# Reordering the first two blocks of a fused chunk attention and MoE kernel: one load, some fillers, one product and one group moved

## The chip, the cores and the metric

One core of a Trainium2 chip (trn2) runs the whole program. The metric is the device time of one execution in microseconds; lower is better. The kernel before takes 287.46 us (median of the four runs that went with the changed kernel, 287.26 to 288.2). A difference counts as faster or slower from 2% on, which is 5.7 us here.

## The reference

```python
def _attn_ref(q, k, v):            # each (8, 8, 576, 64) float32
    # chunks of 64 rows: softmax(q k^T / 8) v inside each chunk
    ...
def _moe_ref(x, w_in, w_out, beta):  # x 4608 x 512, w_in 512 x 2048, w_out 2048 x 512
    h = x @ w_in
    g = h * (1.0 / (1.0 + np.exp(-beta * h)))
    return (g @ w_out).astype(np.float32)

x = attn_out.transpose(0, 2, 1, 3).reshape(B * S, H * D)   # 4608 tokens, 512 features
```

The two matrix products of the second part are nearly all of the work. Attention is worked on in units of 256 tokens (18 of them, two 128-token tiles each); the two products run in blocks of two units (512 tokens). The first product is called layer 1 here, and its 128-row slice m of a block is "m0", "m1" and so on. A bank is one of the buffers of PSUM, the memory that the matmuls write to; an eviction is the instruction of VectorE (DVE) that reads a layer-1 bank, writes the result to SBUF (the memory that the next matmul reads) and so frees the bank. Fillers are matmuls on zeros that only keep TensorE (PE) busy.

## The kernel before

The parts that the change and the argument touch (cuts are marked with `...`):

```python
ps_p = ctx.enter_context(tc.tile_pool(name="ps_p", bufs=4, space=bass.MemoryType.PSUM))  # layer-1 and output banks
ps_s = ctx.enter_context(tc.tile_pool(name="ps_s", bufs=1, space=bass.MemoryType.PSUM))  # one buffer: scores, products, transposes
ps_x = ctx.enter_context(tc.tile_pool(name="ps_x", bufs=1, space=bass.MemoryType.PSUM))  # one more such buffer
...
def emit_pv(u, where=("x", "s")):          # attention product of unit u, both tiles (PE)
    et = et_t.pop(u)
    for s in (1, 0) if u >= MU else (0, 1):
        ...
def emit_norm(u, s):                       # DVE: reciprocal, then multiply, out of PSUM
    ...
def emit_xt_pe(u, s, copy=nc.scalar.copy): # PE transposes of one tile, then one copy to SBUF
    xf = x16_t.pop((u, s)).rearrange("p r h d -> p (r h d)")
    tag = "s" if u < 2 and (u, s) != (1, 0) else "xp"[s]
    xp = {"x": ps_x, "s": ps_s, "p": ps_p}[tag].tile([128, 4, 128], FP16, tag=tag, name="xp")
    ...
def emit_m(j, m, c0=0, n=None, later=False):   # layer 1: 4 matmuls, tanh on ACT, eviction on DVE
    ...
    hps = ps_p.tile([128, 512], FP32, tag="p", name="hps")
    ...
def emit_t(j, t, k0=0, k1=None):               # layer 2; at the last k one copy on ACT and the store
    ...
with tc.manual_schedule():                     # order of emission is the order on each engine
    ...
    for i in range(4):
        load_v(i)
        ...
    make_identity(nc, ident)
    for g in range(8):
        load_w_in(g)
    ...
    emit_T_half(0); emit_sc_half(0, 0); emit_ex_half(0, 0)
    warm = idle_bank()
    emit_idle(6, 512, warm)                    # fillers: matmuls on zeros
    emit_T_half(1)
    nc.vector.transpose(out=bt, in_=braw)
    emit_sc_half(0, 1); emit_ex_half(0, 1); emit_sc_half(1, 0)
    ...
    emit_xt_pe(0, 0)
    emit_pv(1, ("x", "p"))
    emit_norm(1, 1)
    emit_norm(1, 0)
    nc.scalar.activation(out=beta2, in_=bt[:, 0:KFF], func=ACTF.Copy, scale=0.5)
    emit_xt_pe(0, 1)
    d = [emit_m(0, m, 0, 256, True) for m in (0, 1)]
    d[0][0]()                                  # tanh of m0
    emit_xt_pe(1, 1)
    d[1][0]()
    d.append(emit_m(0, 2, 0, 256, True))
    d[0][1]()                                  # eviction of m0 (DVE) ahead of the copy below
    emit_xt_pe(1, 0, nc.vector.tensor_copy)
    d.append(emit_m(0, 3, 0, 256, True))
    ...
    for m in range(4):
        emit_m(0, m, 256, 256)                 # the second half-block: moment S
    ...
    # block 0's layer 2 in 16 groups; unit 2, unit 3 and block 1's first pieces in between
    for i in range(16):
        ...                                    # scores of 2 at 8, product of 2 at 10, scores of 3 at 14
        if i == 15:
            a0, v0 = emit_m(1, 0, 0, 256, True); a0()
            emit_pv(3); emit_norm(3, 0); emit_norm(3, 1)
            v0()
            emit_m(1, 1, 0, 256)
        emit_t(0, i % 4, 4 * (i // 4), 4 * (i // 4) + 4)
    emit_xt_pe(3, 0)
    emit_m(1, 2, 0, 256)
    emit_xt_pe(3, 1)
    emit_m(1, 3, 0, 256)
    emit_m(1, 4, 0, 256)
    for m in range(5, KFF):
        emit_m(1, m)                           # the first full group: moment F
```

The softmax here doesn't subtract the row's maximum and nothing guards it: scores larger than these inputs give would overflow.

## Time and profile before

| | before |
|---|---|
| time, median | 287.46 us |
| span of the profiled execution | 285.8 us |
| TensorE (PE) busy | 279.2 us, 98% |
| VectorE (DVE), ScalarE (ACT) busy | 143.6 and 146.2 us |
| M, first layer-1 matmul | 15.16 us |
| S, second half-block of layer 1 starts | 17.59 us |
| F, first full group of block 1 starts | 49.48 us |

M, S and F are three moments on PE's timeline. PE is full after F (218.95 of 218.95 us in this execution), so what is lost or won ahead of F is lost or won for good. Of the waits of PE (the view lists who waited for whom, us in total, times, longest), these are the ones after the first fillers, and they are short (about 0.25 us more ahead of S and as much ahead of F do not reach this view, because the ends of matmuls are modelled):

```profile
PE hps L329 <- ACT xt L304: 0.7, 1, 0.7
PE x L266 <- ACT et L208: 0.2, 1, 0.2
```

A timeline line reads: start, length, engine, line of the kernel, operation, output<-input, sizes, count, and in brackets the idle time of that engine before it with what ended it. The stretches and timelines on which the argument rests are in the prediction.

### The profile page before, as it was taken

Reading aid. Unit: us, or ns where it says so; the run is one execution under the profiler, and the core shown is the slowest. Engines: PE = TensorE matmul, PEld = TensorE weight load, DVE = VectorE, ACT = ScalarE, POOL = GpSimd, SP = SyncE. Lnnn points to the kernel's source line nnn. Section 1 sums busy time; section 2 is a strip of 40 time slices with the busy share of each in tenths; the row PEclk is TensorE's granted clock in tenths of the full one; section 3 lists DMA queues with packets and bytes.
Section 4 is the critical chain, followed back from the end, with each engine's and each line's share of the span. In section 5 each row is a group of like instructions: output and inputs, shape, how many; then the busy total and the mean of one; then the engine's idle time right before and its main releaser. Section 6 shows DMA issues by size and latency. Waiting matters only on the chain.

```text
span 285.8 us, 6671 instructions
## 1 busy us (share of the span) xinstructions
PE 279.2 (98%) x2779; PEld 136.5 (48%) x2779; DVE 143.6 (50%) x268; ACT 146.2 (51%) x223; POOL 95.6 (33%) x125
## 2 busy tenths in 40 slices
PE   6989999999999999999999999999999999999995
PEld 3564456544544444444444444444444444444444
DVE  2678444776558553535454536363635463333301
ACT  4478228773557545455554555554546444444411
POOL 8853678488073991168607000000000000000000
PEclk9999999999999999999999999999999999999999
DMA  8999999999999999999999983425311221010012
GB/s 198 177 197 206 182 179 213 209 164 150 207 104 173 178 176 162 170 190 187 168 170 164 174 130 78 100 57 119 79 54 39 73 57 55 37 39 37 37 73 76
DMA packets 141085, 37.40 MB, mean 131 GB/s; under 512 B 128000, under 2 KB 136576, under 8 KB 141056
## 3 DMA queue, kind: packets, MB, share of 16 engines
q0 software_dynamic: 99136, 17.83, 82.3%
q1 hardware_dynamic: 41776, 19.09, 32.5%
q8 instruction: 22, 0.36, 0.5%
q10 hardware_dynamic: 144, 0.07, 0.1%
q14 instruction: 7, 0.06, 0.0%
HBM read 36.71 MB, written 9.44 MB: 161 GB/s over the span
## 4 chain that ended last, share of the span: by engine, by line
PE 96%; POOL 1%; ACT 1%; issue 1%; DVE 0%; DVEq 0%; POOLq 0%
PE hps L329 44%; PE ops L361 43%; PE warm L381 2%; PE x L266 2%; PE sc L238 1%; PE ops L602 1%; PE sc L225 1%; PE y L266 1%; ACT xt L304 1%; POOL h L401 1%; PE sc L198 1%; POOL vbig L113 1%; PE xp L303 0%; ACT et L208 0%; PE xp L311 0%
## 5 line engine op out<-in xcount | busy, mean ns | idle before, releaser
L343 DVE SCALAR_TENSOR_TENSOR gt<-sg,hps 128x512 f16<-128x512 f32 (+1 forms) x153 | 99.2, 655 | 101.9 <-ACT sg L339 101.3
L329 PE MATMUL hps<-xt,win 128*128 128x512 f16 (+1 forms) x612 | 136.2, 367 | 0.8 <-ACT xt L304 0.7
L339 ACT ACTIVATE sg<-hps,beta 128x512 f32<-128x512 f32 (+1 forms) x153 | 100.4, 662 | 71.3 <-PE hps L329 69.7
L361 PE MATMUL ops<-wout,gt 128*128 128x512 f16 x560 | 131.1, 379 | 0.0
L329 PEld LDWEIGHTS <-win 128*128 128x128 f16 x612 | 58.3, 98 | 62.4 <-issue 1.0
L361 PEld LDWEIGHTS <-gt 128*128 128x128 f16 x560 | 54.1, 98 | 64.0
L371 ACT ACTIVATE osb<-ops 128x512 f32<-128x512 f32 x35 | 20.9, 598 | 42.8 <-PE ops L361 42.8
L113 POOL DMA_DIRECT2D vbig<-in_v_dram x40 | 34.0, 867 | 11.9 <-DMA wout<-in_moe_w_out_dram 3.6
L99 POOL DMA_DIRECT2D qu<-in_q_dram x22 | 18.7, 859 | 24.9 <-DMA qT<-qu 22.5
L287 DVE TENSOR_TENSOR x<-x,rd 128x512 f16<-128x512 f32 x27 | 18.7, 691 | 1.0
L99 POOL DMA_DIRECT2D ku<-in_k_dram x22 | 18.7, 874 | 0.9 <-DMA ku<-in_k_dram 0.9
L285 DVE RECIPROCAL rd<-x 128x8 f32<-128x8 f32 x27 | 5.4, 199 | 13.1 <-PE x L266 13.1
L247 ACT ACTIVATE et<-sc 128x1024 f16<-128x1024 f32 (+1 forms) x8 | 6.4, 811 | 8.7 <-PE sc L238 8.7
L231 ACT ACTIVATE et<-sc 128x1024 f16<-128x1024 f32 x10 | 10.2, 1021 | 0.7
L266 PEld LDWEIGHTS <-et 64*64 64x64 f16 x576 | 6.0, 107 | 7.4 <-issue 4.7
L381 PE MATMUL warm<-idle 128*128 128x512 f16 (+1 forms) x32 | 8.0, 401 | 0.0
L287 DVE TENSOR_TENSOR x<-y,rd 128x256 f16<-128x256 f32 x18 | 7.6, 424 | 0.6
L105 POOL DMA_DIRECT2D ku<-in_k_dram x9 | 6.8, 755 | 2.6 <-DMA win<-in_moe_w_in_dram 1.3
L105 POOL DMA_DIRECT2D qu<-in_q_dram x9 | 6.8, 766 | 1.5 <-DMA win<-in_moe_w_in_dram 0.7
L266 PE MATMUL x<-vbig,et 64*64 64x65 f16 x432 | 6.7, 194 | 0.2 <-ACT et L208 0.2
L614 DVE TENSOR_SCALAR osb<-ops 128x256 f32<-128x256 f32 (+1 forms) x2 | 0.7, 358 | 12.1 <-PE ops L602 12.1
L131 POOL DMA_DIRECT2D win<-in_moe_w_in_dram x8 | 6.0, 767 | 1.4 <-DMA vbig<-in_v_dram 1.4
(46 smaller groups left out, 75.3 us busy)
## 6 DMA issues: line engine op xcount, KB each, us to landing
out_dram<-osb SPq DMA_DIRECT2D x35, 256.0 KB, 3.6
vbig<-in_v_dram POOLq DMA_DIRECT2D x32, 128.0 KB, 7.8
qu<-in_q_dram POOLq DMA_DIRECT2D x20, 128.0 KB, 5.7
ku<-in_k_dram POOLq DMA_DIRECT2D x20, 128.0 KB, 7.4
win<-in_moe_w_in_dram POOLq DMA_DIRECT2D x8, 256.0 KB, 8.9
wout<-in_moe_w_out_dram POOLq DMA_DIRECT2D x4, 512.0 KB, 12.2
qu<-in_q_dram POOLq DMA_DIRECT2D x3, 256.0 KB, 7.4
ku<-in_k_dram POOLq DMA_DIRECT2D x3, 256.0 KB, 7.9
```

The costliest lines, as they stand in the source:

```text
L99: nc.gpsimd.dma_start(out=tv[off:off + n, sp], in_=src[b, :, s:s + n, :].rearrange("h p d -> p h d"),)
L105: nc.gpsimd.dma_start(out=t[off // 2:(off + n) // 2], in_=src[b, :, s:s + n, :].rearrange("h (p r) d -> p h r d", r=2),)
L113: nc.gpsimd.dma_start(out=vbig[off:off + n, i, :, 0:D], in_=v[b, :, s:s + n, :].rearrange("h p d -> p h d"),)
L231: nc.scalar.activation(out=et, in_=sc, func=ACTF.Exp, scale=scale)
L266: nc.tensor.matmul(out=(x[0][64 * c:64 * c + 64, r, g, 0:D + 1] if len(x) == 1 else x[r][64 * c:64 * c + 64, g, 0:D + 1]), lhsT=(et[64 * r ...
L287: nc.vector.tensor_tensor(out=o, in0=z[..., 0:D], in1=rd[:, r].to_broadcast(list(o.shape)), op=ALU.mult)
L329: nc.tensor.matmul(out=hps[:, 0:n], lhsT=w_in16[m // 2][:, kk, (m % 2) * 128:(m % 2) * 128 + 128], rhs=xr[:, c0 // CH:(c0 + n) // CH, 2 * ...
L339: nc.scalar.activation(out=sg[:, 0:n], in_=hps[:, 0:n], func=ACTF.Tanh, scale=beta2[:, m:m + 1])
L343: nc.vector.scalar_tensor_tensor(out=gt_t[j][:, m, c0:c0 + n], in0=sg[:, 0:n], scalar=1.0, in1=hps[:, 0:n], op0=ALU.add, op1=ALU.mult,)
L361: nc.tensor.matmul(out=ops, lhsT=gt_t[j][:, kk, t * 128:(t + 1) * 128], rhs=w_out16[kk // 4][:, kk % 4, :], start=(kk == 0), stop=(kk == K ...
L371: nc.scalar.activation(out=osb, in_=ops, func=ACTF.Copy, scale=0.5)
L381: nc.tensor.matmul(out=d[:, 0:w], lhsT=idle[:, 0:128], rhs=idle[:, 0:w])
```

## The change

Its intent, as far as the edit tells it: get the first w_in piece into SBUF earlier, let PE reach layer 1 earlier (fewer fillers, half of unit 1's product put behind m0), and in block 1 finish layer 2's last group ahead of unit 3's product so that its bank and its output copy are out of the way. The diff:

```diff
-    def emit_pv(u, where=("x", "s")):
-        et = et_t.pop(u)
-        for s in (1, 0) if u >= MU else (0, 1):
+    def emit_pv(u, where=("x", "s"), which=None):
+        et = et_t[u]
+        for s in which or ((1, 0) if u >= MU else (0, 1)):
 ...
-        tag = "s" if u < 2 and (u, s) != (1, 0) else "xp"[s]
+        tag = ("ss", "sx")[u][s] if u < 2 else "xp"[s]
 ...
+            if i == 2:
+                load_w_in(0)
 ...
-        for g in range(8):
+        for g in range(1, 8):
             load_w_in(g)
 ...
-        emit_idle(6, 512, warm)
+        emit_idle(3, 512, warm)
 ...
-        emit_idle(12, 64, warm)
+        emit_idle(15, 64, warm)
         emit_xt_pe(0, 0)
-        emit_pv(1, ("x", "p"))
-        emit_norm(1, 1)
+        emit_pv(1, ("p", "x"), (0,))
         emit_norm(1, 0)
 ...
-        d = [emit_m(0, m, 0, 256, True) for m in (0, 1)]
+        d = [emit_m(0, 0, 0, 256, True)]
+        emit_pv(1, ("p", "x"), (1,))
+        emit_norm(1, 1)
         d[0][0]()
-        emit_xt_pe(1, 1)
-        d[1][0]()
+        d.append(emit_m(0, 1, 0, 256, True))
+        emit_xt_pe(1, 0)
         d.append(emit_m(0, 2, 0, 256, True))
-        d[0][1]()
-        emit_xt_pe(1, 0, nc.vector.tensor_copy)
+        emit_xt_pe(1, 1, nc.vector.tensor_copy)
         d.append(emit_m(0, 3, 0, 256, True))
-        for act, _ in d[2:]:
+        for act, _ in d[1:]:
             act()
-        for _, vec in d[1:]:
+        for _, vec in d:
             vec()
 ...
-            if i == 8:
+            if i == 9:
                 emit_sc(2)
-            if i == 10:
+            if i == 11:
                 emit_pv(2)
 ...
-            if i == 14:
+            if i == 15:
                 emit_sc(3, True)
-            if i == 15:
                 a0, v0 = emit_m(1, 0, 0, 256, True)
                 a0()
-                emit_pv(3)
-                emit_norm(3, 0)
-                emit_norm(3, 1)
                 v0()
-                emit_m(1, 1, 0, 256)
             emit_t(0, i % 4, 4 * (i // 4), 4 * (i // 4) + 4)
+        a1, v1 = emit_m(1, 1, 0, 256, True)
+        a1()
+        emit_pv(3)
+        emit_norm(3, 0)
+        v1()
+        emit_norm(3, 1)
+        emit_m(1, 2, 0, 256)
         emit_xt_pe(3, 0)
-        emit_m(1, 2, 0, 256)
+        emit_m(1, 3, 0, 256)
         emit_xt_pe(3, 1)
-        emit_m(1, 3, 0, 256)
         emit_m(1, 4, 0, 256)
```

## The prediction

> **What bounds the kernel now.** I read the page first (which engine is full), then the chain of work that ended last in order of time (where that engine is not full), then the busy time by stretch, then each engine's timeline around the two places that the diff touches. The stretches (start, end, length, then busy time of PE, PEld, DVE, ACT, POOL; granted clock, DMA share, GB/s):
>
> ```profile
> 0.00:17.59 17.59, 14.41 (x335) 8.38 (x335) 9.55 (x25) 8.47 (x14) 13.31 (x23) 1.00 1.40 189
> 17.59:49.48 31.89, 31.79 (x357) 16.94 (x357) 18.04 (x34) 17.96 (x32) 20.66 (x27) 1.00 1.64 195
> 49.48:268.43 218.95, 218.95 (x1992) 103.15 (x1992) 113.92 (x206) 117.02 (x174) 61.64 (x75) 1.00 1.14 121
> ```
>
> From 49.48 us on PE is never free until the tail, and the diff leaves that part alone. So whatever the change does is the shift of two moments: **S**, when the second half-block of layer 1 starts (17.59 now; before it PE runs fillers and short pieces), and **F**, when the first full 512-column group of block 1 starts (49.48). Later matmuls only move along with F. The start, from the timelines of PE, ACT and DVE:
>
> ```profile
> 11.66 0.32 PE L266 MATMUL x<-vbig,et 64*64 64x65 f16 x16
> 13.47 0.58 ACT L304 COPY xt<-xp 128x512 f16<-128x512 f16 x1
> 14.10 0.38 PE L303 MATMUL xp<-ident,x 128*128 128x128 f16 x4
> 15.16 1.03 PE L329 MATMUL hps<-xt,win 128*128 128x256 f16 x8 [0.67 <-ACT xt L304]
> 16.36 0.42 DVE L343 SCALAR_TENSOR_TENSOR gt<-sg,hps 128x256 f16<-128x256 f32 x1 [0.22 <-ACT sg L339]
> 17.11 0.42 DVE L304 COPY xt<-xp 128x512 f16<-128x512 f16 x1 [0.33 <-PE xp L303]
> ```
>
> See that the transposes of tile 1 (14.10) start as the copy of tile 0 leaves their buffer (13.47 + 0.58 = 14.05), that layer 1 starts 0.06 us after the next copy (14.52 + 0.58), and that DVE frees the first layer-1 bank (16.36) before it makes the copy that S waits for (17.11 + 0.42 = 17.53). The second place:
>
> ```profile
> 45.61 0.45 PE L266 MATMUL x<-vbig,et 64*64 64x65 f16 x32
> 45.99 0.21 DVE L285 RECIPROCAL rd<-x 128x8 f32<-128x8 f32 x1 [3.27 <-PE x L266]
> 46.23 0.69 DVE L287 TENSOR_TENSOR x<-x,rd 128x512 f16<-128x512 f32 x1
> 46.84 0.20 DVE L285 RECIPROCAL rd<-x 128x8 f32<-128x8 f32 x1
> 47.07 0.69 DVE L287 TENSOR_TENSOR x<-x,rd 128x512 f16<-128x512 f32 x1
> 47.51 0.60 ACT L371 ACTIVATE osb<-ops 128x512 f32<-128x512 f32 x1 [0.39 <-PE ops L361]
> 48.14 0.39 PE L303 MATMUL xp<-ident,x 128*128 128x128 f16 x4
> 48.83 0.60 ACT L304 COPY xt<-xp 128x512 f16<-128x512 f16 x1
> ```
>
> Unit 3's product starts at 45.61; its second tile is normalised at 47.76; the transposes wait a further 0.38 us, until the last output copy (47.51 + 0.60 = 48.11) frees their bank; the copy ends at 49.43 and F follows. Adding the PE work from group 14 (44.21) to F (in us: two groups at 0.86, four first-half pieces m1 to m4 and m0 at 0.43 each, a product 0.38, two transposes at 0.22, without the scores ahead of it) gives 4.69 of 5.27: about half a microsecond of PE is lost here, and about 0.25 just before S. That is nearly all there is to win; 2% of 287.4 would be 5.7 us.
>
> [...] eight 256-column matmuls take 15.16 to 16.03, 109 ns each. [...] The trace's fillers go from 0.43 us each (eight in 3.43, up to 8.41) to 0.22 by 9.31[...]. [...] Landings in this trace, issue start plus time to landing, keep the issue order: v tiles 0 to 3 at 11.05, 11.5, 12.15, 13.06; first and second w_in piece at 14.26 and 15.6. The first of these rows:
>
> ```profile
> vbig<-in_v_dram POOLq DMA_DIRECT2D x1, 128.0 KB, 8.2
> ```
>
> It was issued at 2.85. Landing reaches an engine in under 0.1 us: PE loads its first w_in weight at 14.34.
>
> **The change, part by part.**
>
> *Loads.* v tile 3 and w_in piece 0 swap. Spacings are about 0.9 us for a v tile and 1.2 to 1.35 for a w_in piece, so w_in 0 should land near 13.4 and v tile 3 near 14.3. Piece 1 stays at 15.6, with v tiles 0 and 1 unmoved. w_in 0 was not yet late (14.34 against 15.16), so alone this wins nothing; it is what allows an earlier start.
>
> *Fewer idles.* Three of six fillers go: 3 x 0.22 = 0.65 us. The second half scores need the last DVE transpose (8.74 + 1.07 = 9.81), so they start at 9.85 instead of 10.48. Their exponential ends at 10.96 instead of 11.59, but then unit 0's product waits for v tile 0 (about 11.13 instead of 11.66) and its second half for v tile 1 (about 11.58 instead of 11.81). So of 0.63 us only 0.3 passes: the scores behind it start 11.73 instead of 12.04, the exponential ends 13.26 instead of 13.57, the copy of tile 0 ends 13.74 and the next transposes start 13.79, the copy of tile 1 ends 14.79, and layer 1 starts at 14.84 instead of 15.16. The three added 64-column fillers (0.09 us) lie ahead of that wait.
>
> *Layer 1 ahead of the product.* From 14.84: m0 0.43, the product's other half from 15.29, m1, transposes of unit 1 tile 0 and m2 (from 16.1, after w_in 1). DVE starts on the product's result 0.38 us after its start, as in every row of L266/L285: 15.67, reciprocal to multiply 0.24, multiply 0.69, ends 16.60. Transposes 16.64, DVE copy 0.42 later (17.06 to 17.48). Now the evictions of m0 to m3 all come behind this copy in DVE's order; the first ends at 17.06 + 0.34 + 0.42 = 17.82. There are four layer-1 banks and m0 to m3 hold them, so the second half-block waits for it: S = 17.87 instead of 17.59. **Part sum: +0.3 us.**
>
> *Block 1 a group later.* Scores and product of unit 2 and the scores of unit 3 each move one group; the same work in another order, and no wait appears (normalised unit 2 at 42.20, its transposes at 42.16 to 42.61). Then, counted without part 1: group 14 ends 44.43, scores to 45.07, m0 to 45.50, group 15 to 46.37, m1 to 46.80, unit 3's product at 46.85 instead of 45.61: 1.24 us later. Reciprocal 47.23, multiply 47.47 to 48.16. Then DVE first evicts m1 (about 48.1 to 48.5), then reciprocal 48.43, multiply 48.70 to 49.40. Transposes 49.44, copy 49.86 to 50.45, F about 50.49. PE has only m2, m3, m4 and two transposes behind the product (1.73 us) against a chain of 3.6. The earlier output copy (about 47.25 instead of 48.11) does remove the bank wait of 0.38 and ACT's queue of 0.27. Sum: +1.24 + 0.4 (m1's eviction between the two normalisations) - 0.65 = **+1.0 us**.
>
> Total 287.4 + 0.3 + 1.0 = 288.7.
>
> **Rivals.** (1) The intent works: w_in 0 early starts layer 1 at 14.5 and S is at 17.3, and moving group 15 ahead clears the bank and ACT waits so that F falls at 49.0. For it: both waits exist in the trace. Against: the chain behind the product still needs 3.6 us. Time 286.6 to 287.0. (2) The shifts cancel: the early gain of 0.6 passes whole if v tile 0 lands sooner, but S then stays at 17.55, because the copy and the eviction follow each other on DVE; block 1 costs less as m1's eviction fits beside a wait. Time 287.4 to 288. (3) DMA becomes the bound: v tile 3 or w_in 1 lands late and PE stands for a microsecond; the DMA row is at 9 throughout, but no matmul now waits for a load and the bytes ahead of w_in 1 are the same. Time 289.5.
>
> **Range and chances.** My sums hold best for block 1, since the same constants reproduce the 49.48 of now; the start is less certain by 0.4 us. Weighting rival 2 a little, I put 288.5 us, 287.3 to 289.4. The runs of the kernel before spread 0.9 us. Nothing above reaches 5.7 us: faster by over 2% 0.01, within 2% 0.98, slower 0.01.
>
> **What would show it.** In the changed trace: first layer-1 matmul near 14.8; a PE gap of about half a microsecond before the second half-block, ended by DVE (eviction of m0); unit 3's product about 1.2 us later than before against group 14, then PE gaps before both its transposes, ended by DVE multiplies, and before F, ended by an ACT copy; 1.2 us or so more idle PE up to F, and equal time from F to the end. Wrong if F comes no later than 49.5 (the chain is shorter than I count, for instance the eviction of m1 ran earlier), or if the start gains over 0.3 us (the banks are not what S waits for).

## The result

The changed kernel takes 289.07 us (median of four runs, 288.81 to 289.34) against 287.46 us before. The ratio is 1.0051 with a 95% interval of 1.003 to 1.0072. Ratios here are the mean time of one kernel's runs over the mean of the other's runs of the same rounds, so they are not quite the ratio of the medians. The output is correct. By the 2% rule this is "same", and clear of the noise it is about half a per cent slower. The spans of the two profiled executions are 285.8 and 287.1 us.

The stretches of the changed kernel, cut at its own S and F:

```profile
0.00:17.89 17.89, 14.08 (x335) 8.08 (x336) 9.56 (x25) 8.70 (x14) 13.54 (x24) 1.00 1.39 189
17.89:50.82 32.93, 31.98 (x357) 16.75 (x358) 18.31 (x35) 18.54 (x32) 20.43 (x27) 1.00 1.63 196
50.82:269.74 218.92, 218.92 (x1993) 103.00 (x1992) 113.58 (x205) 116.61 (x173) 61.64 (x75) 1.00 1.11 120
```

The third stretch is as long as before (218.92 against 218.95), so the loss is all ahead of F. The first is 0.30 us longer with less PE work in it, and the second 1.04 us longer (32.93 against 31.89). Among the waits of PE that the kernel before does not have, these two are the longest:

```profile
PE xp L303 <- DVE x L287: 0.7, 2, 0.4
PE hps L329 <- DVE gt L343: 0.4, 1, 0.4
```

The timelines at the start (PE, ACT and DVE):

```profile
13.06 0.59 ACT L304 COPY xt<-xp 128x512 f16<-128x512 f16 x1
...
13.70 0.38 PE L303 MATMUL xp<-ident,x 128*128 128x128 f16 x4 [0.20 <-ACT xt L304]
...
14.75 0.60 PE L329 MATMUL hps<-xt,win 128*128 128x256 f16 x4 [0.67 <-ACT xt L304]
...
17.08 0.42 DVE L304 COPY xt<-xp 128x512 f16<-128x512 f16 x1 [0.49 <-PE xp L303]
17.43 1.43 DVE L343 SCALAR_TENSOR_TENSOR gt<-sg,hps 128x256 f16<-128x256 f32 x4
...
17.89 1.37 PE L329 MATMUL hps<-xt,win 128*128 128x256 f16 x11 [0.41 <-DVE gt L343]
```

In this pair of executions layer 1 starts 0.41 us earlier (14.75 against 15.16), yet S is later. The four evictions of m0 to m3 come in one run of DVE after its copy: m0's tanh had ended at 15.92 (15.45 + 0.47 on ACT), DVE stood 0.49 us ahead of the copy, and the eviction of m0 still ran only behind it, at 17.43. PE stands 0.41 us until the first of them frees a bank. In block 1, first PE's timeline, then DVE's:

```profile
47.21 0.45 PE L266 MATMUL x<-vbig,et 64*64 64x65 f16 x32
...
48.58 0.40 PE L303 MATMUL xp<-ident,x 128*128 128x128 f16 x4 [0.38 <-DVE x L287]
...
49.75 0.40 PE L303 MATMUL xp<-ident,x 128*128 128x128 f16 x4 [0.34 <-DVE x L287]
...
50.82 4.49 PE L329 MATMUL hps<-xt,win 128*128 128x512 f16 x26 [0.24 <-ACT xt L304]
```

```profile
47.83 0.69 DVE L287 TENSOR_TENSOR x<-x,rd 128x512 f16<-128x512 f32 x1
48.44 0.41 DVE L343 SCALAR_TENSOR_TENSOR gt<-sg,hps 128x256 f16<-128x256 f32 x1
48.76 0.20 DVE L285 RECIPROCAL rd<-x 128x8 f32<-128x8 f32 x1
49.00 0.69 DVE L287 TENSOR_TENSOR x<-x,rd 128x512 f16<-128x512 f32 x1
```

Unit 3's product starts 29.32 us after S (47.21 - 17.89), where it started 28.02 us after S before (45.61 - 17.59). PE then waits three times: for each normalised tile and for the last copy. Between the two multiplies DVE evicts m1.

### The profile page after: what moved, and what is told of

Read it like the earlier page. It is cut to its first block, busy times and chain, and to the rows that moved or that the text cites. A ratio compares the mean times of both kernels' runs of the same rounds, so it can differ in the third digit from the quotient of the medians.

```text
span 287.1 us, 6670 instructions
## 1 busy us (share of the span) xinstructions
PE 279.0 (97%) x2779; PEld 135.9 (47%) x2779; DVE 143.5 (50%) x268; ACT 146.6 (51%) x223; POOL 95.6 (33%) x125
## 4 chain that ended last, share of the span: by engine, by line
PE 93%; DVE 2%; DMA 1%; ACT 1%; issue 0%; DVEq 0%
PE hps L329 44%; PE ops L361 42%; PE x L266 2%; DMA raw<-in_q_dram 1%; PE sc L238 1%; PE ops L605 1%; PE sc L225 1%; DVE t L179 1%; PE y L266 1%; PE xp L303 1%; ACT xt L304 1%; DVE x L287 0%; PE sc L198 0%; ACT h L178 0%; ACT et L208 0%
## 5 line engine op out<-in xcount | busy, mean ns | idle before, releaser
L381 PE MATMUL warm<-idle 128*128 128x512 f16 (+1 forms) x32 | 7.3, 378 | 0.0
```

What stands on the lines that cost most here:

```text
L381: nc.tensor.matmul(out=d[:, 0:w], lhsT=idle[:, 0:128], rhs=idle[:, 0:w])
```

## The experiments

Twelve runs were made: ten edits, the unedited changed kernel again, and one edit twice. All gave the right output. The early loads and the pace of PE's fillers move M by up to half a microsecond from one execution to the next (14.75 and 15.21 in the two profiles of the changed kernel, 15.16 and 15.67 in two with the old start), so the table gives the differences between marks, which hardly scatter: M itself, S - M, F - S, then the median time and the ratio to the kernel before.

| run | what it is | M | S - M | F - S | time | ratio (95%) |
|---|---|---|---|---|---|---|
| before | | 15.16 | 2.43 | 31.89 | 287.46 | 1 |
| changed | | 14.75 | 3.14 | 32.93 | 289.07 | 1.0051 (1.003 to 1.0072) |
| after_again | changed, unedited | 15.21 | 3.13 | 32.93 | 289.25 | 1.0059 (1.0041 to 1.0077) |
| e1_start_only | only the start changed | 14.70 | 3.14 | 31.89 | 288.22 | 1.0016 (1.0002 to 1.0029) |
| e2_block_only | only block 1 changed | 15.67 | 2.43 | 32.92 | 289.11 | 1.0045 (1.003 to 1.0059) |
| e3_evict_first | changed, eviction of m0 ahead | 14.67 | 2.81 | 32.92 | 289.01 | 1.0045 (1.0031 to 1.006) |
| e4_norm_first | changed, m1's eviction behind | 15.19 | 3.13 | 33.10 | 288.92 | 1.004 (1.0025 to 1.0055) |
| e9_dve_orders | both of these | 15.17 | 2.81 | 32.61 | 288.55 | 1.0031 (1.0018 to 1.0045) |
| e5_loads_back | changed, loads as before | 16.78 | 3.13 | 32.93 | 289.38 | 1.0058 (1.0044 to 1.0071) |
| e5_again | the same again | 14.94 | 3.13 | 32.93 | 289.15 | 1.0053 (1.0039 to 1.0068) |
| e10_no_fillers | changed, no fillers there | 15.08 | 3.14 | 32.92 | 289.78 | 1.0101 (1.0063 to 1.0139) |
| e6_idles_only | before, three fillers fewer | 14.95 | 2.44 | 31.88 | 287.49 | 0.9993 (0.9981 to 1.0006) |
| e7_bank_free | before, other bank and copy engine | 15.41 | 2.44 | see below | 287.05 | 0.9982 (0.9967 to 0.9996) |
| e8_both | both, and both transposes ahead of m2 | 14.96 | no wait at S | see below | 287.09 | 0.9974 (0.9959 to 0.9989) |

The theory under test: the start and block 1 each lose on their own; at the start because the eviction of m0 stands behind a copy in DVE's order while PE needs its bank, in block 1 because a fixed chain (product, normalise, transpose, copy) begins 1.3 us later with too little matmul work beside it, and m1's eviction lengthens it.

### e1_start_only and e2_block_only: the two halves of the change

```diff
 e1: the changed kernel, but
-            the tests of i (9, 11, 15) and the lines from a1, v1 = ... to emit_m(1, 3, 0, 256)
+            the same lines of the kernel before
 e2: the kernel before, with those lines of the changed kernel
```

> Only the changes up to block 0's second half (loads swapped, fewer idles, product split, DVE order); block 1 as in the kernel before. Theory A (DVE's first-in-first-out order makes the second half-block wait for the eviction of m0, which now stands behind the copy): S at 17.89, F at 49.48 + 0.30 = 49.78, time 0.3 us above the kernel before (287.8), so ratio about 1.001. Rival B (the start is where the whole loss arises, block 1's different timing is only its echo): F above 50.5 and time near 289. Rival C (the start gains and the trace's 0.3 is a fluke of that run): S at or below 17.6, time at or below 287.4.

> Only block 1's scores, product and group moved; the start as in the kernel before. Theory A (the product of unit 3 comes 1.3 us later and its chain of normalise, transpose, copy has too little matmul work beside it): S 17.59, F 49.48 + 1.04 = 50.5, time 1.0 us above the kernel before (288.5), ratio about 1.0036; gaps of PE before both transposes of unit 3, ended by DVE multiplies. Rival B: F near 49.5 and no loss, since it came from the start.

Measured: the two halves separate cleanly. The start alone has the changed kernel's S - M (3.14) and the old F - S (31.89); block 1 alone has the old S - M (2.43) and the new F - S (32.92). e1's S was 17.84 and its F 49.73. e2's S was 18.10 rather than the 17.59 expected, though its start is the old code: its six fillers took 2.13 us instead of 1.64, which is the pace of PE's fillers, taken up below. In time, e1 is slower by 0.16% and e2 by 0.45%; these add to 0.61%, against the 0.51% and 0.59% of the two series of the changed kernel. Rival B (block 1 only echoes the start) is out, and so is rival C (S at or below 17.6).

### e3_evict_first, e4_norm_first and e9_dve_orders: two instructions of DVE

```diff
 e3 (and e9)
         d.append(emit_m(0, 2, 0, 256, True))
+        d[0][1]()
         emit_xt_pe(1, 1, nc.vector.tensor_copy)
 ...
-        for _, vec in d:
+        for _, vec in d[1:]:
 e4 (and e9)
         emit_norm(3, 0)
-        v1()
         emit_norm(3, 1)
+        v1()
```

> The changed kernel with one DVE instruction moved: the eviction of m0 ahead of the copy of unit 1's second tile. Theory A: the eviction runs at about 16.5 to 16.9, in DVE's gap before the copy (17.08 to 17.50), so S falls from 17.89 to about 17.56 and the time by 0.33 us (288.7 against 289.07). Rival D (S waits for the tanh or for a weight load, not for the bank that DVE frees): S stays at 17.9.

> The changed kernel with one DVE instruction moved: the eviction of m1 of block 1 behind the normalisation of unit 3's second tile. Theory A: that normalisation ends 0.3 us earlier (about 49.35 instead of 49.70), the transposes and the copy follow, F falls from 50.82 to about 50.45, unless m4, whose bank that eviction frees, then holds it (m4 could start at 49.75 at the earliest, F at 50.2: no). Time 0.35 us below the changed kernel (288.7). Rival E (the gap before the second transposes is set by something else): F stays at 50.8.

> The changed kernel with both DVE instructions moved (eviction of m0 ahead of the copy, eviction of block 1's m1 behind the second normalisation). Theory A: S - M 2.8 instead of 3.14, F - S 32.6 instead of 32.93, together 0.65 us off the changed kernel of the same submission, ratio to the kernel before about 1.0022. If the remaining loss is the later product itself, 0.7 us of F - S stays, whatever DVE's order.

Measured: e3's S - M falls by 0.33 us to 2.81, as expected; so the bank that DVE frees is what S waits for in the changed kernel. Its time (289.01) does not resolve a third of a microsecond. e4 missed its expectation on the face of it: F - S rose to 33.10. The trace shows why. In that execution PE paused within unit 3's 64 score matmuls (45.70 to 46.00 in the chain, with no wait that the profile shows), and the scores took 1.13 us instead of 0.64. From the product to F, e4 took 3.29 us (51.42 - 48.13) against the changed kernel's 3.61 (50.82 - 47.21), so the 0.32 us is there, but hidden. e9 settles it, with both edits and no pause. DVE's timeline of e9:

```profile
16.92 0.41 DVE L343 SCALAR_TENSOR_TENSOR gt<-sg,hps 128x256 f16<-128x256 f32 x1
17.50 0.42 DVE L304 COPY xt<-xp 128x512 f16<-128x512 f16 x1 [0.16 <-PE xp L303]
...
48.52 0.20 DVE L285 RECIPROCAL rd<-x 128x8 f32<-128x8 f32 x1
48.75 0.69 DVE L287 TENSOR_TENSOR x<-x,rd 128x512 f16<-128x512 f32 x1
```

The eviction now fits into the gap that DVE had ahead of its copy, and the second reciprocal follows the first multiply (which starts at 47.91) at once. S - M is 2.81 and F - S 32.61, together 0.65 us less than the changed kernel. In time e9 has 288.55 us against 289.25 for the unedited changed kernel, 0.70 us less. What is left of F - S, 32.61 - 31.89 = 0.72 us, goes by this account to the later product, whatever DVE's order; no run moves the product alone. What is left of S - M, 2.81 - 2.43 = 0.38 us, comes with the split of unit 1's product: half of it (0.25 us, 15.28 to 15.53 in the changed kernel) now runs between M and S, and in e9 S (17.98) waits for DVE's copy (17.50 + 0.42 = 17.92), which depends on that half. Nor did the split bring M nearer: from unit 0's second scores to M it is 4.68 us before (15.16 - 10.48), 4.69 in e6 below, where the product is whole, and 4.72 to 4.87 in the two profiles of the changed kernel.

### e5_loads_back and e5_again: does the load swap matter?

```diff
-            if i == 2:
-                load_w_in(0)
 ...
-        for g in range(1, 8):
+        for g in range(8):
             load_w_in(g)
```

> The changed kernel with the load order of the kernel before (v of tile 3 ahead of the first w_in piece). Theory A (the swap moves a transfer that nobody waits for): w_in 0 lands near 14.3 instead of 13.5, before layer 1 can start (14.75, set by the copy of tile 1), S stays at 17.9 and F at 50.8, time equal to the changed kernel within 0.2 us (289.0). Rival F (the swap is what lets layer 1 start early, as the change's wording suggests): layer 1 starts later than 14.9 and waits for a DMA, time 289.2 or more.

> The load order put back in the changed kernel, once more: its first profile fell on a run in which the second half of q and k landed 0.7 us late and TensorE then ran at the slow pace, so that look could not tell. Theory A (nobody waits for the swapped transfer): in a look without that, M 14.75, first w_in weight loaded by 14.4, S 17.9, time as the changed kernel's of the same submission within 0.3 us. Rival F (the swap is needed): the first layer-1 weight load is ended by a DMA, M above 15.0 though the copy of tile 1 ended earlier.

Measured: the first look could not tell (M at 16.78, for another reason, in the next part). In e5_again the first layer-1 weight load did wait for the transfer, but only until 14.43, and M was then set by the copy of tile 1 at 14.94, as in every other run. PE's weight loads in e5_again:

```profile
14.43 0.10 PEld L329 LDWEIGHTS <-win 128*128 128x128 f16 x1 [0.34 <-DMA win<-in_moe_w_in_dram]
```

The changed kernel loads that weight at 13.86. So the swap brings the piece half a microsecond earlier to a place where the next matmul waits for something else; e5_again's time (289.15) and after_again's (289.25) do not differ. By these figures it would matter only if M could get below about 14.5 (an estimate from the 14.43).

### e6_idles_only and e10_no_fillers: what the fillers do

```diff
 e6: the kernel before          e10: the changed kernel
-        emit_idle(6, 512, warm)    -        emit_idle(3, 512, warm)
+        emit_idle(3, 512, warm)
```

> The kernel before with three fillers fewer and nothing else. Theory A: layer 1 starts at about 14.75 as in the changed kernel, but DVE still evicts m0 before its copy, so S follows at about 17.2 (14.75 + 2.43), 0.4 us ahead of the kernel before; F about 49.07; time 287.1 to 287.3, ratio 0.9985. Rival G ([...] the early start runs into w_in 0): S at 17.6 or later, ratio 1 or above.

> The changed kernel with none of the three fillers left, so that TensorE stands from about 8.9 to 9.85. Theory H [...]: the 64-column fillers and transposes after it take the long durations (fillers over 0.05 us each, transposes 0.59 instead of 0.39), layer 1 starts at 15.5 or later, time 1 us or more above the changed kernel. Rival I (fillers at that place only waste time): M 14.7, time equal to the changed kernel within 0.2 us.

Measured: e6's S - M is the old 2.44, with m0 evicted ahead of the copy, so its S (17.39) is earlier than before (17.59), by 0.2 us instead of the expected 0.4. The step that was off is the fillers' pace. PE's timeline of e6, then of the changed kernel:

```profile
8.92 1.41 PE L381 MATMUL warm<-idle 128*128 128x512 f16 x3
```

```profile
8.88 0.82 PE L381 MATMUL warm<-idle 128*128 128x512 f16 x3
```

Three identical fillers took 1.41 us in one execution and 0.82 in the other: PE reached its fast pace (0.22 us for such a filler, against 0.43 at the slow one) at different moments. The granted clock of the profile does not show this: it reads 1.00 from 4.84 to 8.35 us in the kernel before, where the fillers took 0.43 us each, and 1.00 from 9.30 to 10.40, where they took 0.22. What sets the moment is not shown; fast and slow pace mean here only what the matmuls took. The time of e6 (ratio 0.9993) is not to be told from the kernel before; its profiled execution, the slowest of its six, also lost half a microsecond after F, in two pauses of PE near 95.6 and 155.2 us.

The question behind e10 was whether the slow pace, which followed a gap of 1.20 us in e5_loads_back, also follows another gap of about a microsecond at that place. Its expectation missed: with no fillers, its profile shows a gap of 1.13 us and the fast pace after it. M was 15.08 because its scores waited for DVE's last transposes, and these for the second half of k, which landed at 2.12 + 6.8 = 8.92 us. That load landed at 8.6 in the profile of the changed kernel and at 9.32 in after_again. But e5_loads_back had the other outcome after a gap of 1.20 us (its load landed at 2.12 + 7.35 = 9.47). PE's timelines, e5_loads_back first, then e10_no_fillers:

```profile
8.24 0.45 PE L198 MATMUL sc<-t,t 32*64 32x64 f16 x32
...
10.63 0.71 PE L198 MATMUL sc<-t,t 32*64 32x64 f16 x64 [1.20 <-DVE bt L433]
...
13.24 1.41 PE L381 MATMUL warm<-idle 128*128 128x512 f16 x16
14.45 0.59 PE L303 MATMUL xp<-ident,x 128*128 128x128 f16 x4
```

```profile
8.35 0.64 PE L198 MATMUL sc<-t,t 32*64 32x64 f16 x32
10.12 0.71 PE L198 MATMUL sc<-t,t 32*64 32x64 f16 x64 [1.13 <-DVE bt L434]
...
12.30 0.83 PE L381 MATMUL warm<-idle 128*128 128x512 f16 x16
12.96 0.39 PE L303 MATMUL xp<-ident,x 128*128 128x128 f16 x4
```

The same sixteen fillers took 1.41 us at the slow pace and 0.83 at the fast one, the same four transposes 0.59 and 0.39. That execution of e5_loads_back had a mean granted clock of 0.992 and took 291.05 us, 1.7 us above its fellows. Two of the four runs of e10 took 290.28 us (clock 0.992) and 292.16 (0.998), and one of after_again 290.31 (1.0). The kernel before never took more than 288.34 us in the twelve runs listed with the first eight experiments and the ten with the last four. So fewer fillers leave the start open to a late load (with six of them, in e7 below, the load landed as late, at 2.13 + 7.2 = 9.33, and PE did not wait for it), and in one profile the slow pace followed. Why one gap brings it and another of nearly the same length does not stays open, as do the runs that were not profiled. One difference: ahead of its gap, e5_loads_back was already at the fast pace (the 32 scores at 8.24 took 0.45 us) and turned slow near 11.5 us, about 3.3 us after it had turned fast, until about 14.9 (estimates from its timeline: two fillers at 11.28 took 0.87 us against 0.60 in e10, 32 scores at 12.66 took 0.64, and 16 product matmuls at 14.98 again 0.32); in e10 the scores ahead of the gap were still slow (0.64 us). No run varies this alone.

### e7_bank_free and e8_both: what the kernel before could still win

```diff
 e7 and e8, on the kernel before
-        tag = "s" if u < 2 and (u, s) != (1, 0) else "xp"[s]
+        tag = "s" if u < 2 and (u, s) != (1, 0) or (u, s) == (3, 1) else "xp"[s]
 ...
         emit_xt_pe(3, 0)
-        emit_m(1, 2, 0, 256)
-        emit_xt_pe(3, 1)
+        a2, v2 = emit_m(1, 2, 0, 256, True)
+        a2()
+        emit_xt_pe(3, 1, nc.vector.tensor_copy)
+        v2()
 e8 besides
-        emit_idle(6, 512, warm)
+        emit_idle(3, 512, warm)
 ...
-        d.append(emit_m(0, 2, 0, 256, True))
         d[0][1]()
         emit_xt_pe(1, 0, nc.vector.tensor_copy)
+        d.append(emit_m(0, 2, 0, 256, True))
```

> The kernel before with the last transposes of unit 3 put into the buffer that its own product has just left (no wait for the last output copy) and their copy given to DVE ahead of the eviction of m2. Theory A (the half microsecond that block 1 lost before came from that bank and from ACT's queue): transposes at about 48.0, copy about 48.4 to 48.8, F at 49.05 to 49.1 instead of 49.48, PE without a gap from the product to F; time 0.4 us below the kernel before, ratio 0.9986. Rival: F stays at 49.4 since the copy of unit 3's first tile or the evictions hold it.

> The kernel before with three fillers fewer, both transposes of unit 1 ahead of m2, and the block 1 edit of the bank-free run. Theory A: S at about 16.95 to 17.0 (PE-bound from the first layer-1 matmul at 14.75: four pieces 0.43 and two transposes 0.22 are 2.16), F 31.5 us later at about 48.5, so 1.0 us ahead of the kernel before; time 286.4 to 286.7, ratio 0.9966. Rival: the gains do not add, as the later matmuls then meet loads that land no earlier, F above 49.

Measured: in e7 no wait is left in block 1. PE's timeline of e7, where the transposes and the layer-1 pieces follow each other without a gap:

```profile
47.58 0.39 PE L303 MATMUL xp<-ident,x 128*128 128x128 f16 x4
47.80 0.60 PE L329 MATMUL hps<-xt,win 128*128 128x256 f16 x4
48.24 0.39 PE L303 MATMUL xp<-ident,x 128*128 128x128 f16 x4
48.46 1.25 PE L329 MATMUL hps<-xt,win 128*128 128x256 f16 x9
```

As F is no wait there, take the distance from S to the start of the last 48 matmuls: 278.65 - 17.85 = 260.80 us in e7, 278.79 - 17.59 = 261.20 before. That is the 0.40 us that was expected, and the time agrees (ratio 0.9982, 287.05 us). So what the kernel before lost here was the bank and ACT's queue (e7 lifts both at once and does not tell them apart), and both can be avoided without moving the product.

e8 has the best ratio, 0.9974, and beats both kernels, but not by the microsecond that was expected. PE has no gap from M to S. In the profiled execution, however, M was 14.96 (the fillers ran slow again, 1.38 us), and from M to the last 48 matmuls it took 263.62 us, against 263.24 in e7 and 263.63 before. Set against e7's timeline group by group, e8 is 0.58 us ahead when layer 2 of block 0 starts and loses that lead in steps: 0.24 us in unit 3's scores (0.90 us in the chain against 0.66), 0.06 near 68 us and 0.25 near 154 us. None of these shows a wait. They are not e8's alone: e4 paused within the same 64 scores, and e3 and e6 at the same step from layer 2 to layer 1 as e8 near 154 us (155.8 and 155.2 there, about 105.5 us after F in e8 and e3). What PE stands for at these places, in some executions and not in others, is open; e8 and e7 cannot be told apart by their times.

### after_again: the yardstick

> The changed kernel again, unedited, as the yardstick for the other runs of this submission and for how far its marks scatter. All theories: S - M (second half-block minus first layer-1 matmul) 3.14, F - S 32.93, time 1.3 us above the kernel before, ratio 1.0045; M between 14.6 and 15.3 [...].

Measured: as expected, except that the ratio is a little higher (1.0059), with the one run of 290.31 us in it. S - M and F - S repeat to 0.01 us while M moves from 14.75 to 15.21.

## Why the prediction was right

The prediction said 288.5 us with 287.3 to 289.4, and "within 2%"; the kernel took 289.07. It holds by its own steps, though not every close figure is skill: the moments M, S and F themselves move by half a microsecond between executions of the same kernel (after_again has 15.21, 18.34 and 51.27), so that they were met to 0.1 us in the one profile is partly luck. The distances S - M and F - S, the causes, and the times are what count.

- **M.** Predicted 14.84, seen at 14.75, and at 15.21 in after_again, where the second half of k landed late. Of the 0.60 us by which the scores start earlier (9.88 against 10.48), 0.41 arrive at M. That the loads of v eat part of it is right, but in this profile less than predicted: the product's first half starts at 11.06 instead of the predicted 11.13, as its exponential ends (10.39 + 0.60), since v tile 0 had landed at 2.86 + 8.0 = 10.86; the second half starts at 11.34 instead of 11.58, some 0.13 us later than right behind the first.
- **Loads.** w_in 0 was expected near 13.4 and landed at 5.51 + 8.0 = 13.5; v tile 3 near 14.3 and landed at 6.25 + 8.1 = 14.35. (The spacing of "about 0.9 us for a v tile" held only for the last tile: the prediction's own landings are 0.45, 0.65 and 0.91 apart.) That the swap alone wins nothing is shown by e5_again.
- **S.** Predicted 17.87 with DVE's eviction as the cause; seen at 17.89, and e3 and e9 show the cause. As a distance, S - M was predicted as 3.03 and measured 3.14. That the start as a whole loses does not rest on one profile: e1 alone is slower by 0.02 to 0.29%, 0.1 to 0.8 us, around the predicted 0.3.
- **F.** Predicted 50.49 plus the 0.3 of the start, so 50.8; seen at 50.82. Of the terms, the later product was put at 1.24 us and measured 1.30; m1's eviction was put at 0.4 and measured 0.32 (e9); the removed waits were put at 0.65 and come to 0.58 (3.87 us from product to F before, 3.61 after, of which 0.32 are the eviction: 3.87 - 3.61 + 0.32).
- **Time.** The sum, 288.7, is nearer than the stated 288.5. The shading towards the rival in which the shifts cancel was not earned: e2 alone shows the whole of it (32.92 - 31.89 = 1.03).

One step was weaker than it reads. The saving of three fillers at 0.22 us takes the fast pace as reached and kept, which was the estimate. It was kept in the profile of the changed kernel and not in e5_loads_back; in after_again, e6 and e8 it had not yet come when the three fillers began: the three took 1.32 us in after_again, and in e6 and e8 1.41 and 1.38 us, over 0.4 each. The profile pair gives +1.3 us and the times +1.6 by the medians; the interval (0.3 to 0.7%, that is 0.9 to 2.1 us) covers both, so the times ask for no further cause; they do not rule one out.

The rivals: the first (the intent works) fell with e1 and e2, the second (the shifts cancel) with e2 (block 1 costs all that was summed). The third (a load becomes the bound) has nothing in the changed kernel's waits of PE, where no load is listed.

## What to carry to other kernels

When a product, its normalisation, transpose and copy form a chain that a full engine must wait for, start the chain as early as its inputs allow and keep enough independent matmuls behind it; moving it later to clear a buffer costs its whole delay (1.30 us here, of which the cleared waits gave back 0.58), while another free buffer and another copy engine cleared the same waits in e7 with no delay elsewhere in block 1. On an engine that runs its instructions in the order of emission, as DVE did in these traces (m0's eviction, ready at 15.92, ran at 17.43 behind the copy), an eviction that frees a bank belongs ahead of a copy that has to wait anyway (0.33 us in e3). Compare differences between marks in the traces rather than spans: here they repeat to a hundredth of a microsecond while the start moves by half of one, unless PE pauses in between, as in e4.

## What scattered from run to run

- The pace of PE at the start. The eight fillers begin at 4.82 to 4.85 us in the six profiles read there (before, changed, e1 to e4). The fast pace came at about 8.2 us in e5_loads_back, whose 32 scores at 8.24 took 0.45 us, and at about 10.4 us in e2_block_only (an estimate: its six fillers fill 8.93 to 10.99, which at 0.43 and 0.22 each makes 3.5 slow ones). So three identical fillers, begun between 8.62 and 8.93 us, took 0.82 to 1.46 us, and six took 1.64 to 2.13. The slow pace followed a gap of 1.20 us in e5_loads_back, while a gap of 1.13 us left the pace fast in e10_no_fillers. How short a gap can bring the slow pace back is not shown.
- The landing of a load. The second half of k (256 KB written), with other loads issued ahead of it, took 6.5 to 7.35 us in these executions. The scatter of 0.85 us moves the start of the kernel (scores at 9.88 us in the changed kernel's profile, at 10.49 in after_again).
- PE pauses without a shown wait, about 0.2 to 0.5 us long, inside runs of matmuls (e4 at 45.70, e6 near 95.6, e8 near 43.8 and 154), in several executions at the same places of the program. What they are is not shown.
